# A fused linear-attention and squared-ReLU kernel: the order of the first 16 microseconds rewritten

## The chip, the cores and the metric

The kernel runs on one core of one Trainium2 chip. The metric is device time in microseconds (us) for one execution. The core has five engines with queues of their own: TensorE (PE in the profile; PEld is its weight load), VectorE (DVE), ScalarE (ACT), GpSimd (POOL) and SyncE (SP), which issues most of the DMAs. Each works through its own list of instructions in order and waits on semaphores for the others.

## The reference

```python
x = A_x                                  # 1 x 2048 x 448, bf16
xn = _layernorm(x, axis=-1)
s = _A_ref(xn, A_wqkv, A_wo)             # 16 heads of 28, linear attention
g = _silu(_B_ref(xn, B_w1, B_b1, B_w2, B_b2))
return x + s * g

# _A_ref: q, k, v from xn @ wqkv; phi(t) = where(t > 0, t + 1, exp(t)) + 1e-6
#   num = phi(q) (phi(k)^T v), den = phi(q) . sum phi(k); o = num / den; o @ wo
# _B_ref: h = xn @ w1 + b1; r = max(h, 0)^2; r @ w2 + b2       (448 -> 1792 -> 448)
```

## The kernel before

The 2048 tokens lie on 128 partitions as 16 tiles of 128; four tiles make a group g. The 448 features are three blocks of 128 rows and a tail of 64 rows. The hidden layer h of the second branch has 1792 columns in 14 chunks of 128 (index `fi`). Weights w1 come in four pieces of 512 columns (`load_w1(p)`), each as one load of the three full blocks, `("w1", p, 0)`, and two small loads of the 64-row tail, `("w1", p, 1)` and `("w1", p, 2)`, one in each half of the partitions. Two 64-row matmuls on different halves run side by side.

No loop order is left to a compiler. The program records operations (`add`) with what they read and write, an estimated duration and an engine. TensorE and SP keep the order in which the operations were recorded. For VectorE, ScalarE and GpSimd, `schedule` makes the order: of the operations that can start soonest it takes the one with the lowest `late`, its due time, worked back from TensorE's needs, or `prio` where one is set (lower goes first; within `pr.hot` operations get a rising series from -100). It also gives each accumulator (`Buf`) one of eight PSUM banks, the one that comes free soonest in its own estimate. The order is then fixed; on the chip an engine waits where the estimate was too early.

The head works as follows. For chunks 0 to 7 of group 0, h is computed from raw x, since the layer norm's mean and deviation can be put in afterwards. `warm` runs 34 dummy matmuls on zeros. `raw_transpose(lo)` turns two raw x tiles by TensorE into PSUM; VectorE and ScalarE copy two feature blocks each into `xr`. `pe_part(us, part, need)` multiplies chunks 0 to 3 for one half (256 tokens) of the group: 12 full-height matmuls and 4 of the 64-row tail. `col_sums(p)` sums the columns of w1 on TensorE; ScalarE (`csh`) and VectorE (`csl`) put them in a row form. `ln_stats`, `ln_rstd` and `ln_norm` are the layer norm: mean and variance on VectorE, Ln and Exp on ScalarE, the normalised tile `xn` on VectorE. `x_transpose` then copies the tail once more (VectorE) and issues a DMA transpose into `xT` on SP, two tiles at a time; all work after chunk 7 uses `xT`. `stat_rows` writes mean and deviation of the first four tiles into `rows`, `row_transpose` turns them on TensorE, and VectorE copies them to `rowT`. `aug` adds the product of `csl` and `rowT` to each accumulator of h, which puts mean and bias right, and hands the chunk to ScalarE (relu) and VectorE or ScalarE (square). `pe_two(a, b)` computes two chunks whole, with their tails side by side; `pe_main` and `pe_tails` are its two pieces.

The recorded order of TensorE in the head is: dummies, raw transposes of tiles 0 and 1, of 2 and 3, the two parts of chunks 0 to 3, column sums of pieces 0 and 1, chunks 4 and 6, row transpose, full blocks of chunk 5, augmentation of chunks 0 to 3, full blocks of chunk 7, tails of 5 and 7, augmentation of chunks 4 to 7, a transpose of b1, and then K (`kk`, with `phi`) and further chunks of h over `xT`. SP's recorded order is: x tiles 0 to 3, w1 piece 1, x tiles 4 to 7, b1, the k columns of wqkv, w1 piece 2, the two DMA transposes of tiles 0 to 3, the q columns (3 loads), w1 piece 3 (3 loads), x tiles 8 to 11, the transposes of tiles 4 to 7, x tiles 12 to 15, w2 and the rest. ScalarE issues w1 piece 0 and the row of b1.

Some lines of the profile: L425 DMA loads, L482 and L483 statistics, L490 and L494 Ln and Exp, L501 normalise, L510 tail copy, L515 DMA transpose, L614 and L621 phi on VectorE, L631 K, L653 Q, L680 and L683 relu, L688 square, L707 partial matmuls, L710 whole raw chunks, L711 chunks over `xT`, L731 to L734 raw transposes, L741 and L746 their copies, L767 to L776 column sums, L784 and L789 `csh` and `csl`, L803 to L826 `rows`, L842 row transpose, L849 its copy, L856 augmentation, L1193 dummies, L1247 and L1248 b1's transpose and copy.

Of the kernel before, what the change touches and what calls it, by code (L numbers as in the profile page):

```python
# [9 lines left out]
P = 128  # L10
S, D, F = 2048, 448, 1792
# [17 lines left out]
class Op:  # L29
    def __init__(self, eng, emit, reads, writes, dur, alts, nbytes):  # L30
        self.eng, self.emit, self.dur, self.alts, self.nbytes = eng, emit, dur, alts, nbytes
        self.reads, self.writes = list(reads), list(writes)
        self.raw, self.deps, self.succ = set(), set(), []
        self.start = self.end = None
        self.seq = None
        self.late = 1e9
        self.prio = None
        self.sync = None
        self.fence = False
        self.fixed = 0.0  # L40


class Program:
# [42 lines left out]
    def schedule(self):  # L86
# [34 lines left out]
        def ready(op):  # L121
            r = 0.0
            for d in op.deps:
                if d.end is None:
                    return None
                r = max(r, d.end + LAT)
            return r

        def bank_time(b):
# [11 lines left out]
        n = len(ops)  # L141
# [146 lines left out]
def bass_recurrent_scan__linear_attn_block__dense_activation_squared_relu__prompt_kernel(  # L288
    nc, A_x, A_wqkv, A_wo, B_x, B_w1, B_b1, B_w2, B_b2, out
):  # L290
    with ExitStack() as es:
# [3 lines left out]
        add = pr.add  # L295
# [128 lines left out]
        def dma(eng, dst, src, writes, nbytes, reads=(), dur=0.45):  # L424
            op = add(eng, lambda e, _: e.dma_start(dst, src), reads, writes, dur, nbytes=nbytes)  # L425
            if eng == "act":
                op.prio = -1000.0 + len(pr.ops)

        def load_x(lo, hi, eng="sp"):
            dma(eng, x_tok[:, lo:hi, :], tok(A_x, lo, hi), [("x", i) for i in range(lo, hi)], (hi - lo) * P * D * 2)  # L430

        def load_k(eng, w, src, name, lo, hi):
# [12 lines left out]
        def load_w1(p, eng, eng2):  # L445
            lo, hi = 512 * p, min(512 * p + 512, F)
            m = (hi - lo) // 2
            dma(
                eng, w_1[:, :, lo:hi], B_w1[0:384, lo:hi].rearrange("(c p) j -> p c j", p=P), [("w1", p, 0)],
                768 * (hi - lo),  # L450
            )
            for i in (0, 1):
                dma(
                    eng2, w_1r[64 * i : 64 * i + 64, 256 * p : 256 * p + m],
                    B_w1[384:448, lo + m * i : lo + m * i + m], [("w1", p, 1 + i)], 128 * m,
                )

        w1names = lambda p: [("w1", p, i) for i in range(3)]

# [3 lines left out]
        dma("act", b1row[:, :], B_b1.rearrange("(o f) -> o f", o=1), ["b1row"], F * 2)  # L463
        load_w1(1, "sp", "sp")
        load_x(4, 8)
        dma("sp", b1r[:, :], B_b1.rearrange("(f p) -> f p", p=P), ["b1r"], F * 2)
        load_k("sp", w_qkv, A_wqkv, "wk", D, 2 * D)
        load_w1(2, "sp", "sp")

        def late_loads():  # L470
# [10 lines left out]
        def ln_stats(si):  # L481
            add("dve", lambda e, _: e.bn_stats(st6[:, si, :], x_tok[:, si, :]), [("x", si)], [("st", si)], 0.58)  # L482
            add("dve", lambda e, _: e.bn_aggr(mv[:, si, :], st6[:, si, :]), [("st", si)], [("mv", si)], 0.15)  # L483

        def ln_rstd(lo, hi):
            c = slice(lo, hi)
            ts = range(lo, hi)
            add(
                "act",
                lambda e, _: e.activation(out=vep[:, c], in_=mv[:, c, 1], func=AF.Ln, bias=eps5[:, 0:1]),  # L490
                [("mv", i) for i in ts] + ["eps5", "actw"], [("vep", i) for i in ts], 0.25,
            )
            add(
                "act", lambda e, _: e.activation(out=rstd[:, c], in_=vep[:, c], func=AF.Exp, scale=-0.5),  # L494
                [("vep", i) for i in ts], [("rstd", i) for i in ts], 0.2,
            )
# [89 lines left out]

        def pe_part(us, part, need):
            def f(e, _):
                for u in us:
                    for k in range(3):  # L590
                        u[2](e, slice(0, 128), k, k == 0, False, part)
                for i in (0, 1):
                    us[i][2](e, slice(0, 64), 3, False, False, part)
                    last = us[2 + i][2](e, slice(64, 128), 3, False, False, part)
                return last

            banks = [u[0] for u in us]
            add("pe", f, list(need) + us[0][1] + (banks if part else []), banks, 14 * MM(256) + 0.1)

        def pe_tails(a, b, close=True):  # L600
            def f(e, _):
# [93 lines left out]
        def hh(g, fi, full=True):  # L695
            b = Buf("H")

            def mm(e, rw, c, start, stop, part=None):
                if c < 3:
                    lhs = w_1[rw, c, fi * P : (fi + 1) * P]  # L700
                else:
                    lhs = w_1r[rw, rest_col(fi) : rest_col(fi) + P]
                if raw(g, fi):
                    src = xr[rw, c, :]
                    if part is not None:
                        t = slice(256 * part, 256 * part + 256)
                        return e.matmul(  # L707
                            ps(b)[:, t], lhs, src[:, t], start=start and part == 0, stop=False, skip_group_check=True
                        )
                    return e.matmul(ps(b)[:, 0:512], lhs, src, start=start, stop=stop)  # L710
                return e.matmul(  # L711
                    ps(b)[:, 0:512], lhs, xT[rw, 4 * g : 4 * g + 4, c, :], start=start, stop=stop
                )
# [41 lines left out]
        def col_sums(p):  # L755
# [4 lines left out]
            def f(e, _):  # L760
# [22 lines left out]
            add(  # L783
                "act", lambda e, _: e.activation(out=csh[0:n, w : w + P], in_=ps(b)[0:n, w : w + P], func=AF.Copy), [b],  # L784
                [("csh", p)], 0.3,
            ).prio = -50
            add(
                "dve",
                lambda e, _: e.scalar_tensor_tensor(  # L789
# [4 lines left out]
            ).prio = -50  # L794

        def stat_rows():
            mvs = [("mv", i) for i in range(4)]
# [14 lines left out]
                ),  # L812
                mvs + ["rows0"], ["rows1"], 0.12,
            )
            add(
                "act",
                lambda e, _: e.activation(out=sdev[:, :], in_=vep[:, 0:4], func=AF.Exp, scale=0.5),
# [8 lines left out]
                lambda e, _: e.tensor_tensor(out=rows[:, :, :, 4], in0=sd4, in1=rows[:, :, :, 3], op=ALU.subtract),  # L826
                ["sdev", "rows3"], ["rows4"], 0.12,
            )
            add(
                "act",  # L830
                lambda e, _: e.activation(out=rvar[:, :], in_=vep[:, 0:4], func=AF.Exp, scale=-1.0),
# [3 lines left out]
        def row_transpose():  # L835
            b = Buf("R")

            def f(e, _):
                v = ps(b)[:, :].bitcast(bf)
                last = None  # L840
                for k in range(4):
                    last = e.transpose(  # L842
                        v[:, k * P : (k + 1) * P], rows[:, k, :, :].rearrange("p r j -> p (r j)"), ident[:, :]
                    )
                return last

            add("pe", f, ["rows1", "rows4", "ident"], [b], 0.3)
            v = ps_bf(b)
            add("dve", lambda e, _: e.tensor_copy(rowT, v()[:, 0:512]), [b], ["rowT"], 0.42).prio = -60  # L849

        def aug(units, fis, skip=False):
            def f(e, _):
# [287 lines left out]
        def ss_last(early, mid):  # L1140
# [43 lines left out]
            main(1)  # L1184
            main(2)

        def warm(n, after=()):
            b = Buf("W")

            def f(e, _):  # L1190
                last = None
                for _i in range(n):
                    last = e.matmul(ps(b)[:, 0:P], wz[:, :], wz[:, :], start=True, stop=True)  # L1193
                return last

            add("pe", f, ["wz", *after], [b], n * 0.06)

        def quads(what):
            us = []
# [6 lines left out]
            if us:  # L1206
                pe_two(*us)

        def ln(lo, hi, stats=True, step=2, lead=0.0):
            pr.lead = lead  # L1210
            if stats:
                for si in range(lo, hi):
                    ln_stats(si)
            ln_rstd(lo, hi)
# [132 lines left out]
```

## Time and profile before

| | us |
|---|---|
| median of 9 runs | 154.95 |
| lowest and highest | 154.56, 155.53 |
| the profiled execution | 154.95 |
| its span, first to last instruction | 153.2 |

The span leaves 1.75 us of the profiled execution's time outside. The granted clock of TensorE averages 1.000 over the span.

| engine | busy us | share of the span | instructions |
|---|---|---|---|
| PE | 146.5 | 96% | 1093 |
| DVE | 96.6 | 63% | 237 |
| ACT | 78.4 | 51% | 149 |
| POOL | 35.4 | 23% | 54 |

A row of the timeline has the start, the length, the engine, the line, the operation, its output and inputs, and how many were merged; in brackets the idle time of the engine before it and what ended that. The length of a merged row runs to the end of its last instruction; matmuls overlap, so the distance from start to start is what one costs. A row of the chain of waits has start, length and what it was. A busy share by slice is in tenths.

### The profile page before, as it was taken

Reading aid. Unit: us, or ns where it says so; the run is one execution under the profiler, and the core shown is the slowest. Engines: PE = TensorE matmul, PEld = TensorE weight load, DVE = VectorE, ACT = ScalarE, POOL = GpSimd, SP = SyncE. Lnnn points to the kernel's source line nnn. Section 1 sums busy time; section 2 is a strip of 40 time slices with the busy share of each in tenths; the row PEclk is TensorE's granted clock in tenths of the full one; section 3 lists DMA queues with packets and bytes.
Section 4 is the critical chain, followed back from the end, with each engine's and each line's share of the span. In section 5 each row is a group of like instructions: output and inputs, shape, how many; then the busy total and the mean of one; then the engine's idle time right before and its main releaser. Section 6 shows DMA issues by size and latency. Waiting matters only on the chain.

```text
span 153.2 us, 2797 instructions
## 1 busy us (share of the span) xinstructions
PE 146.5 (96%) x1093; PEld 69.4 (45%) x1093; DVE 96.6 (63%) x237; ACT 78.4 (51%) x149; POOL 35.4 (23%) x54
## 2 busy tenths in 40 slices
PE   7799999999999999999999999989999999999990
PEld 7564343444434444344443554434444545454450
DVE  2497959999998876364789510087954423414573
ACT  1531986887959598273969214979231021111100
POOL 7860004465000055000550000000005505133100
PEclk9999999999999999999999999999999999999999
DMA  4999799970007070000000000000001111010132
GB/s 114 334 277 135 191 257 307 319 163 7 0 0 135 2 140 1 0 0 4 0 2 2 4 0 0 0 4 0 0 0 46 44 34 60 0 60 0 60 109 71
DMA packets 17994, 11.05 MB, mean 72 GB/s; under 512 B 9469, under 2 KB 17597, under 8 KB 17982
## 3 DMA queue, kind: packets, MB, share of 16 engines
q1 hardware_dynamic: 17420, 10.42, 26.7%
q10 hardware_dynamic: 562, 0.46, 0.9%
q8 instruction: 8, 0.13, 0.3%
q14 instruction: 4, 0.03, 0.1%
HBM read 6.95 MB, written 1.84 MB: 57 GB/s over the span
## 4 chain that ended last, share of the span: by engine, by line
PE 72%; DVE 16%; DMA 5%; SPq 3%; ACT 1%; issue 1%; DVEq 0%
PE pb L1061 27%; PE pb L711 17%; PE pb L875 6%; DMA x_tok<-in_A_x_dram 5%; PE pb L1115 5%; PE pb L631 4%; PE pb L653 3%; DVE r L688 3%; DVE pk L621 3%; DVE st L482 3%; SPq L425 2%; PE pb L707 2%; DVE pqT L621 2%; DVE pk L614 2%; PE pb L1120 1%; DVE pqT L614 1%
## 5 line engine op out<-in xcount | busy, mean ns | idle before, releaser
L1061 PE MATMUL pb<-w,r 128*128 128x448 bf16 x224 | 44.8, 353 | 0.0
L711 PE MATMUL pb<-xT,w 64*128 64x512 bf16 (+1 forms) x264 | 36.9, 377 | 0.5 <-DVE kvm L915 0.4
L683 ACT ACTIVATE r<-pb,b1f 128x512 bf16<-128x512 f32 x48 | 29.7, 692 | 7.9 <-PE pb L711 7.8
L1061 PEld LDWEIGHTS pb<-w,r 128*128 128x128 bf16 x224 | 20.8, 98 | 20.9 <-issue 2.1
L688 DVE TENSOR_TENSOR r<-r 128x512 bf16<-128x512 bf16 x37 | 17.2, 501 | 12.1 <-ACT r L683 12.1
L1101 ACT ACTIVATE gbuf<-gbuf 128x448 bf16<-128x448 bf16 x15 | 8.6, 581 | 29.6 <-DVE gbuf L1091 29.6
L641 POOL TENSOR_TENSOR zacc<-zacc,pk 128x448 f32<-128x448 f32 x13 | 14.6, 1121 | 39.0 <-DVE pk L621 35.7
L1134 POOL TENSOR_TENSOR obuf<-obuf,x_tok 128x448 bf16<-128x448 bf16 x10 | 10.1, 1029 | 52.8 <-DVE obuf L1131 52.8
L711 PEld LDWEIGHTS pb<-xT,w 64*128 64x128 bf16 (+1 forms) x264 | 13.3, 94 | 17.9 <-issue 1.2
L1091 DVE TENSOR_TENSOR gbuf<-pb,b2b 128x448 bf16<-128x448 f32 x11 | 6.9, 625 | 16.1 <-PE pb L1061 16.0
L631 PE MATMUL pb<-w_qkv,xT 64*128 64x448 bf16 x112 | 13.2, 350 | 0.3 <-DVE b1f L1248 0.3
L1131 DVE TENSOR_TENSOR obuf<-pb,gbuf 128x448 bf16<-128x448 f32 x14 | 8.3, 621 | 5.3 <-PE pb L1120 5.2
L609 ACT ACTIVATE pk<-pb 128x448 bf16<-128x448 f32 x16 | 7.9, 548 | 7.1 <-PE pb L631 7.1
L482 DVE BATCH_NORM_STATS2 st<-x_tok 128x6 f32<-128x448 bf16 x16 | 9.5, 615 | 3.0 <-DMA x_tok<-in_A_x_dram 3.0
L689 ACT ACTIVATE r<-r 128x512 bf16<-128x512 bf16 x19 | 11.2, 643 | 0.0
L653 PE MATMUL pb<-xT,w_qkv 64*128 64x512 bf16 (+1 forms) x72 | 10.0, 377 | 0.3 <-DVE pk L621 0.3
L621 DVE SCALAR_TENSOR_TENSOR pk<-pb,pk 128x448 bf16<-128x448 f32 x16 | 9.6, 619 | 0.3
L875 PE MATMUL pb<-pk,xn 128*128 128x448 bf16 x48 | 9.4, 353 | 0.0
L711 PE MATMUL pb<-xT,w_1r 64*128 64x512 bf16 x48 | 9.1, 378 | 0.0
L1115 PE MATMUL pb<-msb,pqT 128*128 128x448 bf16 x42 | 9.1, 353 | 0.0
L631 PEld LDWEIGHTS pb<-w_qkv,xT 64*128 64x128 bf16 x112 | 5.2, 94 | 6.5 <-issue 0.7
L621 DVE SCALAR_TENSOR_TENSOR pqT<-pb,pqT 128x512 bf16<-128x512 f32 x12 | 8.0, 685 | 0.2
(127 smaller groups left out, 142.4 us busy)
## 6 DMA issues: line engine op xcount, KB each, us to landing
out_dram<-obuf SPq DMA_DIRECT2D x15, 112.0 KB, 1.7
w<-in_B_w_dram SPq DMA_DIRECT2D x1, 1568.0 KB, 10.3
x_tok<-in_A_x_dram SPq DMA_DIRECT2D x3, 448.0 KB, 5.4
w_qkv<-in_A_wqkv_dram SPq DMA_DIRECT2D x3, 336.0 KB, 5.6
w<-in_B_w_dram SPq DMA_DIRECT2D x2, 384.0 KB, 6.3
x_tok<-in_A_x_dram SPq DMA_DIRECT2D x2, 224.0 KB, 3.8
w_o<-in_A_wo_dram SPq DMA_DIRECT2D x1, 392.0 KB, 10.0
w<-in_B_w_dram ACTq DMA_DIRECT2D x1, 384.0 KB, 4.2
```

The lines of the kernel that those rows point to most:

```text
L482: add("dve", lambda e, _: e.bn_stats(st6[:, si, :], x_tok[:, si, :]), [("x", si)], [("st", si)], 0.58)
L621: lambda e, _: e.scalar_tensor_tensor(out=slot, in0=ps(buf)[:, 0:n], scalar=1.0 + 1e-6, in1=slot, op0=ALU.add, op1=ALU.max),
L631: return e.matmul(ps(b)[:, 0:D], xT[rw, si, c, :], w_qkv[rw, c, D : 2 * D], start=start, stop=stop)
L641: lambda e, _: e.tensor_tensor(out=o[:, :], in0=pk[:, 0, :] if i == 1 else zacc[:, :], in1=pk[:, i, :], op=ALU.add),
L653: return e.matmul(ps(b)[:, 0:512], w_qkv[rw, c, m * P : (m + 1) * P], xT[rw, 4 * g : 4 * g + 4, c, :], start=start, stop=stop,)
L683: rl = lambda e, _: e.activation(out=slot, in_=ps(b)[:, 0:512], func=AF.Relu, bias=b1f[:, fi : fi + 1])
L688: return e.tensor_tensor(out=slot, in0=slot, in1=slot, op=ALU.mult)
L689: return e.activation(out=slot, in_=slot, func=AF.Square)
L711: return e.matmul(ps(b)[:, 0:512], lhs, xT[rw, 4 * g : 4 * g + 4, c, :], start=start, stop=stop)
L875: last = e.matmul(ps(b)[:, 0:D], xn[:, si, c * P : (c + 1) * P], pk[:, si, :], start=(si == 0), stop=(si == NT - 1),)
L1061: last = e.matmul(ps(bb[fi >= 8])[:, 0:D], r2[:, fi, si * P : (si + 1) * P], w_2[:, fi, :], start=(fi == 0 and part is None) or (g == 0 an ...
L1115: last = e.matmul(ps(b)[:, 0:D], pqT[:, c, si * P : (si + 1) * P], msb[:, c, :], start=(c == 0), stop=False)
```

## The change

The diff does the following.

- `warm` issues 38 dummies instead of 34, always on one accumulator, and its estimate for the planner is 0.1 us each.
- `pe_part` does only the 12 full-height matmuls and waits only for the main load of w1 piece 0. The tails of chunks 0 to 3 follow as two `pe_tails` pairs over all 512 tokens, after the second part.
- TensorE's order behind that is: column sums of piece 0, row transpose, column sums of piece 1, augmentation of chunks 0 to 3, chunks 4 and 6 whole, chunks 5 and 7 whole, augmentation of chunks 4 to 7.
- The statistics of all four tiles of group 0 are recorded first, then `stat_rows` (with one Ln over four tiles), then the Exp for the normalisation, over four tiles, then the normalisations and both DMA transposes. In `stat_rows` the deviation comes ahead of that Exp and the variance's Exp behind it.
- The priorities of `csh` and `csl` go from -50 to -150, that of `rowT` from -60 to -200.
- The statistics of tiles 4 to 7 get a `hold`: the planner starts them no earlier than the copy of `rowT`.
- On SP the load of b1 comes behind the k columns. `load_w1r` is split off `load_w1`. Two further helpers (`load_x2`, `load_w1a`) are defined and not called.

```diff
             for d in op.deps: ...
+            for d in op.hold:
+                if d.end is None:
+                    return None
+                r = max(r, d.start)
...
         load_x(4, 8)
+        load_k("sp", w_qkv, A_wqkv, "wk", D, 2 * D)
         dma("sp", b1r[:, :], B_b1.rearrange("(f p) -> f p", p=P), ["b1r"], F * 2)
-        load_k("sp", w_qkv, A_wqkv, "wk", D, 2 * D)
...
         def pe_part(us, part, need):
             def f(e, _):
+                last = None
                 for u in us:
                     for k in range(3):
-                        u[2](e, slice(0, 128), k, k == 0, False, part)
-                for i in (0, 1):
-                    us[i][2](e, slice(0, 64), 3, False, False, part)
-                    last = us[2 + i][2](e, slice(64, 128), 3, False, False, part)
+                        last = u[2](e, slice(0, 128), k, k == 0, False, part)
                 return last
-            add("pe", f, list(need) + us[0][1] + (banks if part else []), banks, 14 * MM(256) + 0.1)
+            add("pe", f, list(need) + [("w1", 0, 0)] + (banks if part else []), banks, 12 * MM(256) + 0.1)
...
+            ln_vep(0, 4)
             add("act", ... sdev ...)
             add("dve", ... rows3 ...)
             add("dve", ... rows4 ...)
+            ln_rstd(0, 4, False)
             add("act", ... rvar ...)
...
-        warm(34)
+        warm(38)
         raw_transpose(0)
         raw_transpose(2)
         pe_part([H0[i] for i in range(4)], 0, [("xr", 0, 0), ("xr", 0, 1)])
         pr.hot = -100.0
-        for si in (0, 2):
-            ln(si, si + 2)
+        for si in range(4):
+            ln_stats(si)
         stat_rows()
+        ln(0, 4, stats=False, rstd=False)
         pr.hot = None
         pe_part([H0[i] for i in range(4)], 1, [("xr", 2, 0), ("xr", 2, 1)])
+        pe_tails(H0[0], H0[2], close=False)
+        pe_tails(H0[1], H0[3], close=False)
         col_sums(0)
+        rt = row_transpose()
         col_sums(1)
+        aug([H0[i] for i in range(4)], range(4), True)
         pe_two(H0[4], H0[6], close=False)
-        row_transpose()
-        pe_main(H0[5])
-        aug([H0[i] for i in range(4)], range(4), True)
-        pe_main(H0[7])
-        pe_tails(H0[5], H0[7], close=False)
+        pe_two(H0[5], H0[7], close=False)
         aug([H0[i] for i in range(4, 8)], range(4, 8))
...
-        ln(4, 8, lead=3)
+        ln(4, 8, lead=3, hold=[rt])
```

More of the change, by code (lines that the diff above doesn't have):

```diff
@@ L40, in __init__ @@
         self.fixed = 0.0
+        self.hold = ()
 class Program:
@@ L430, in load_x, with load_x2, load_w1a, load_w1r @@
             dma(eng, x_tok[:, lo:hi, :], tok(A_x, lo, hi), [("x", i) for i in range(lo, hi)], (hi - lo) * P * D * 2)
+        halves = (("sp", slice(0, 64)), ("act", slice(64, P)))
+        def load_x2(lo, hi):
+            for i, (eng, r) in enumerate(halves):
+                dma(
+                    eng, x_tok[r, lo:hi, :], tok(A_x, lo, hi)[r], [("x", k, i) for k in range(lo, hi)],
+                    (hi - lo) * 64 * D * 2,
+                )
+            for k in range(lo, hi):
+                pr.alias(("x", k), [("x", k, 0), ("x", k, 1)])
+        def load_w1a():
+            for i, (eng, r) in enumerate(halves):
+                dma(
+                    eng, w_1[r, :, 0:512], B_w1[0:384, 0:512].rearrange("(c p) j -> p c j", p=P)[r],
+                    [("w1", 0, 0, i)], 384 * 512,
+                )
+            pr.alias(("w1", 0, 0), [("w1", 0, 0, 0), ("w1", 0, 0, 1)])
+        def load_w1r(p, eng2):
+            lo, hi = 512 * p, min(512 * p + 512, F)
+            m = (hi - lo) // 2
+            for i in (0, 1):
+                dma(
+                    eng2, w_1r[64 * i : 64 * i + 64, 256 * p : 256 * p + m],
+                    B_w1[384:448, lo + m * i : lo + m * i + m], [("w1", p, 1 + i)], 128 * m,
+                )
         def load_k(eng, w, src, name, lo, hi):
@@ L451, in load_w1 @@
             )
-            for i in (0, 1):
[L453 to L456, printed above, removed]
+            load_w1r(p, eng2)
         w1names = lambda p: [("w1", p, i) for i in range(3)]
@@ L479, in bass_recurrent_scan__linear_attn_block__dense_activation_squared_relu__prompt_kernel, with ln_stats, ln_vep @@
         late_constants()
-        def ln_stats(si):
-            add("dve", lambda e, _: e.bn_stats(st6[:, si, :], x_tok[:, si, :]), [("x", si)], [("st", si)], 0.58)
+        def ln_stats(si, hold=()):
+            op = add("dve", lambda e, _: e.bn_stats(st6[:, si, :], x_tok[:, si, :]), [("x", si)], [("st", si)], 0.58)
+            op.hold = hold
             add("dve", lambda e, _: e.bn_aggr(mv[:, si, :], st6[:, si, :]), [("st", si)], [("mv", si)], 0.15)
-        def ln_rstd(lo, hi):
+        def ln_vep(lo, hi):
             c = slice(lo, hi)
@@ L492, in ln_rstd @@
             )
+        def ln_rstd(lo, hi, vep_=True):
+            c = slice(lo, hi)
+            ts = range(lo, hi)
+            if vep_:
+                ln_vep(lo, hi)
             add(
@@ L588, in f @@
             def f(e, _):
+                last = None
                 for u in us:
                     for k in range(3):
-                        u[2](e, slice(0, 128), k, k == 0, False, part)
-                for i in (0, 1):
-                    us[i][2](e, slice(0, 64), 3, False, False, part)
-                    last = us[2 + i][2](e, slice(64, 128), 3, False, False, part)
+                        last = u[2](e, slice(0, 128), k, k == 0, False, part)
                 return last
             banks = [u[0] for u in us]
-            add("pe", f, list(need) + us[0][1] + (banks if part else []), banks, 14 * MM(256) + 0.1)
+            add("pe", f, list(need) + [("w1", 0, 0)] + (banks if part else []), banks, 12 * MM(256) + 0.1)
         def pe_tails(a, b, close=True):
@@ L709, in mm @@
                         )
-                    return e.matmul(ps(b)[:, 0:512], lhs, src, start=start, stop=stop)
+                    return e.matmul(ps(b)[:, 0:512], lhs, src, start=start, stop=stop, skip_group_check=fi < 4)
                 return e.matmul(
@@ L785, in col_sums @@
                 [("csh", p)], 0.3,
-            ).prio = -50
+            ).prio = -150
             add(
@@ L793, in col_sums @@
                 [b, ("csh", p), "rmask"], [("csl", p)], 0.28,
-            ).prio = -50
+            ).prio = -150
         def stat_rows():
@@ L848, in row_transpose @@
             v = ps_bf(b)
-            add("dve", lambda e, _: e.tensor_copy(rowT, v()[:, 0:512]), [b], ["rowT"], 0.42).prio = -60
+            op = add("dve", lambda e, _: e.tensor_copy(rowT, v()[:, 0:512]), [b], ["rowT"], 0.42)
+            op.prio = -200
+            return op
         def aug(units, fis, skip=False):
@@ L1185, in ss_last @@
             main(2)
+        wb = Buf("W")
         def warm(n, after=()):
-            b = Buf("W")
             def f(e, _):
@@ L1192, in f @@
                 for _i in range(n):
-                    last = e.matmul(ps(b)[:, 0:P], wz[:, :], wz[:, :], start=True, stop=True)
+                    last = e.matmul(ps(wb)[:, 0:P], wz[:, :], wz[:, :], start=True, stop=True)
                 return last
-            add("pe", f, ["wz", *after], [b], n * 0.06)
+            add("pe", f, ["wz", *after], [wb], n * 0.1)
         def quads(what):
@@ L1207, in quads, with ln @@
                 pe_two(*us)
-        def ln(lo, hi, stats=True, step=2, lead=0.0):
+        def ln(lo, hi, stats=True, rstd=True, step=2, lead=0.0, hold=()):
             pr.lead = lead
@@ L1212, in ln @@
                 for si in range(lo, hi):
-                    ln_stats(si)
-            ln_rstd(lo, hi)
+                    ln_stats(si, hold)
+            if rstd:
+                ln_rstd(lo, hi)
             for si in range(lo, hi, step):
```

## The prediction

> **What bounds the kernel now.** I read the busy shares by slice first, then the chain of waits that ended last, then the first 25 us instruction by instruction.
>
> ```profile
> PE   7799999999999999999999999989999999999990
> DVE  2497959999998876364789510087954423414573
> ```
>
> (The slices are 3.83 us each.) TensorE looks like the bound everywhere, so time taken out of the head would seem to shorten the whole. But VectorE is full in the slices from 23 to 46 us as well. The chain, cut to 17 to 44 us (start, length, what), says which of the two sets the time there:
>
> ```profile
> 17.75 3.83 DMA x_tok<-in_A_x_dram
> 21.57 0.02 issue
> 21.59 0.63 DVE st L482
> 22.22 0.36 DVE pk L614 x2
> 22.58 1.06 DVE pk L621 x2
> ...
> 43.26 0.05 issue
> 43.31 0.82 PE pb L711 x5
> ```
>
> From 21.59 to 43.26 us the chain stays on VectorE, and TensorE takes it over only at 43.31. What starts it is the load of x tiles 8 to 11 that SP issues at 17.75. The same chain before that (12 to 18 us) runs over SP's queue: the second normalised-x transpose (12.78 to 14.08), then seven loads behind it, each 0.49 to 0.60. So between 13 and 43 us there are two nearly equal bounds. TensorE's last matmul before 43.31 starts at 42.85 and a 512-column matmul takes 0.216 (start to start in this trace), so TensorE alone would be there at 43.07: only 0.24 us of slack. After 43 us VectorE has idle time and the chain is TensorE's.
>
> The wait in question, in the timeline of VectorE and TensorE:
>
> ```profile
> 21.59 0.63 DVE L482 BATCH_NORM_STATS2 st<-x_tok 128x6 f32<-128x448 bf16 x1 [1.54 <-DMA x_tok<-in_A_x_dram]
> 23.17 0.98 PEld L653 LDWEIGHTS pb<-xT,w_qkv 128*128 128x128 bf16 x6 [0.75 <-DVE pk L621]
> ```
>
> VectorE sat 1.54 us idle because the planner put tile 8's statistics ahead of the first two k tiles' phi; the first Q matmuls then waited for the second of these for 0.41 us (0.63 start to start against 0.216).
>
> **The head, part by part.** The rows I use:
>
> ```profile
> 7.68 1.47 PE L707 MATMUL pb<-xr,w 128*128 128x256 bf16 x12 [0.79 <-ACT xr L746]
> 9.09 0.39 PE L707 MATMUL pb<-xr,w_1r 64*128 64x256 bf16 x4
> 14.31 0.42 DVE L849 COPY scr<-pb 128x512 bf16<-128x512 bf16 x1 [0.84 <-PE pb L842]
> 15.30 1.09 ACT L680 ACTIVATE r<-pb 128x512 bf16<-128x512 f32 x2 [2.75 <-PE pb L856]
> 10.24 3.83 SPq L515 DMA_TRANSPOSE xT<-xn  x2
> ```
>
> *Dummies, 34 to 38.* The trace grants the full clock from 4.15 us, 3.10 after the first dummy; the last dummies are 0.055 apart, the early ones 0.107. Four more cost 0.22 by the row. [...]
>
> *Tails out of the partial matmuls.* The row of the first part names ScalarE, but its sequencer stood until 7.52 at two DMA semaphores: the 64-row remainder of w1, landed at 7.48. The new part waits for the main w1 load (landed 5.02) and the copies of xr (ScalarE's, 0.60, done at about 6.35). It then follows the raw transposes: last one issued 6.65, plus 0.21 for the change of shape (as at 9.08), so 6.86 instead of 7.68. Twelve matmuls at 0.109 twice give 9.48. Tails cost 0.42 a part now (8.99 to 9.41), 0.84 together; two 512-column pairs cost 0.10 + 0.22 + 0.32 (13.45 to 13.56, one pair, 13.56 to 13.88) = 0.64. Column sums of chunks 0 to 3 start at about 10.13 (now 11.15), end at 10.63.
>
> *Statistics rows.* All four tiles' statistics come first. VectorE reaches the last at 8.55 as now; its aggregate ends near 9.37 (now 10.05). Then ScalarE, from the rows at 10.09 to 10.8: Ln to 9.71, deviation to 9.94. VectorE: rows3 to 10.18, by the planner's rule one normalisation (0.38), rows4 to 10.7. The row transpose runs at 10.75, its copy 11.2 to 11.62, the first column-sum row (0.35) to 11.9, and the early augmentation at 12.0 (copy to matmul is 0.12 now). TensorE, done with the second column sums at 11.48, waits 0.5 us here, and the pairs of chunks 4 to 7 stand behind that wait though they could run; today they cover it. So what the head gains before 10.75 isn't all passed on. If rows4 goes ahead of, or behind one more, normalisation: 11.7 or 12.4.
>
> *Early augmentation, both pairs whole.* After 12.0 + 0.32: two blocks of 1.73 (as 12.15 to 13.88), the second augmentation 0.23, b1's transpose 0.2: first K matmul at about 16.2, now 16.97 (that block now holds the row transpose 0.23, the wait for its copy, two augmentations, and a wait for b1f of 0.32 because its bank is reused; four banks are free by then). ScalarE's relu begins near 12.5, not 15.30. Gain on TensorE 0.75 at K, 0.84 behind it (0.09 of waiting on relu goes), and 1.25 at the first Q if its 0.41 goes too.
>
> *Normalised x.* Here the change takes something back. Its first two tiles wait for all four statistics and the row copy: the first DMA transpose is released at about 12.1 (now 10.24), the second at 12.83. SP issues in order. One takes 1.30 to 1.35 us at best (rows at 12.78, 18.38, 47.27), 2.48 at worst (10.24, while loads filled the queue until 13.39). I take the low end, since that 2.48 ended at 12.72, when the loads were nearly through: 12.1 + 1.33 + 0.05 + 1.30 = 14.78, now 14.08. [...] The rows decide: SP comes 0.70 late. Landing (1.85 after the issue) 16.6, needed at 17.0 by the first H over xT; 0.4 of slack. Behind it on SP are three wq, three w1 and x tiles 8 to 11: these land near 22.3, not 21.57. Statistics of tiles 4 to 7 (10.45 to 15.80 now) are held until the row copy and then run from about 13.0 to 15.4: no loss, for their transposes stand behind the x load on SP anyway. Moving b1r behind wk moves a 3.5 KB load and costs nothing.
>
> **The sum.** TensorE alone gains 1.25. VectorE: restart 0.70 later, but what it has left then is less. With relu finished by 18.3 the two exponentials of K come at 18.3 to 19.3, not 19.57 to 20.6, and the planner, which puts x 8 to 11 near 21 us in its own times, then finds K's phi ready first. That is 0.36 + 1.06 = 1.42 us of VectorE work (chain lines above) moved into the idle time. Net 1.42 - 0.70 = 0.72 at 43.31, the smaller gain, and it carries to the end. The profiled execution took 154.95 (span 153.2 and 1.75 around it), which is also the median: **154.2**.
>
> **Rivals.**
> *TensorE's whole gain* (1.25, 153.7): VectorE's full stretch holds work that nothing is waiting for yet (1.59 us of later statistics at 38.20, squares); a better order could hide it. Against it: no gap in 21 us.
> *Given back* (154.95): the planner reorders all that follows and 0.7 us is two fillers in a bad place.
> *SP's late x load makes it slower*: if the first transpose's issue takes 2.48 again, the second ends at 15.93, x 8 to 11 land 1.85 late, and even with phi first the sum is 1.85 - 1.42 = 0.43 worse, 155.4. If the planner leaves the statistics first, 0.70 late means 155.65. It decides from the point where the second transpose's issue ends later than 14.08 + 1.42 = 15.50. For it: the chain runs through that queue today.
> *The dummies don't matter*: already open at 4.15 in this execution; then nothing changes in the sum, as it counts nothing for them.
>
> **Numbers.** The sum as worked out 0.42 (its own range 153.9 to 154.6); whole gain 0.16; given back 0.15; slower by SP 0.27. Runs of this kernel can tell about 0.2% (0.31 us). Faster 0.42 + 0.16 = 0.58, same 0.15, slower 0.27. Range 153.4 (0.3 beyond the whole gain, for waits that go elsewhere) to 155.7.
>
> **What would show it.** First partial matmul near 6.9; column sums near 10.1; early augmentation near 12.0; first K near 16.2; second transpose's issue ends near 14.8; VectorE's statistics of tile 8 after the first two phi, with the wait for Q gone; the chain's change from VectorE to TensorE near 42.6. I am wrong if x tiles 8 to 11 land after 23, if these statistics still stand ahead of phi, or if the clock opens after the raw transposes.

## The result, and the profile after

The changed kernel takes 153.52 us (median of 12 runs, 153.44 to 154.49); the kernel before, timed beside it, 154.88. The ratio is 0.9918, with a 95% interval of 0.9900 to 0.9936: 1.36 us by the medians. In the profiled executions it is 1.44 (154.95 to 153.51; spans 153.22 and 151.78). The forecast was 154.2, a gain of 0.75; its range holds the result close to its lower end. The direction and the head came out as worked out; the gain is nearly twice the forecast. The outcome that lay nearest was "TensorE's whole gain", 153.7. A profile is of one execution, and executions of one kernel differ by 1 us and more (153.44 to 154.49 for the changed kernel, 154.49 to 156.37 for the one before), so a start read from a profile is weighed against the spans of all its runs.

The page of the changed kernel, busy shares by slice (3.79 us each), and the shares of its chain of waits:

```profile
PE   7999999999999999999999999989999999999990
...
DVE  2489849999997875455789310196954432414573
...
PE 96%; DVE 2%; ACT 0%; issue 0%; DVEq 0%
```

TensorE's second slice is full now. VectorE still has six slices at 9 from 23 us on, and yet the chain has 2% of VectorE in it, where the chain before had 16% (and 72% of TensorE). The stretch on VectorE from 21.59 to 43.26 has left the chain, although VectorE does nearly the same work there. The chain of the changed kernel in that stretch (start, length, what):

```profile
11.26 0.42 DVE scr L885
11.69 0.27 DVE scr L823
...
21.95 1.72 PE pb L687 x8
...
40.96 4.97 PE pb L745 x36
```

Only the copy of the row transpose (L849 before, L885 now) and the first column-sum row (L789, now L823) stand between matmuls; from 12 us to beyond 45 there is nothing but TensorE. The timeline of the head answers the rows of before (line numbers moved by 30 to 40):

```profile
7.00 2.79 PE L741 MATMUL pb<-xr,w 128*128 128x256 bf16 x24
...
12.00 0.39 PE L894 MATMUL pb<-scr 32*128 32x512 bf16 x4 [0.27 <-DVE scr L823]
12.08 2.72 SPq L551 DMA_TRANSPOSE xT<-xn  x2
...
12.45 2.06 ACT L714 ACTIVATE r<-pb 128x512 bf16<-128x512 f32 x4 [0.39 <-PE pb L894]
...
16.10 0.93 PE L665 MATMUL pb<-w_qkv,xT 64*128 64x448 bf16 x8
...
19.71 1.15 DVE L655 SCALAR_TENSOR_TENSOR pk<-pb,pk 128x448 bf16<-128x448 f32 x2
...
21.88 1.79 PE L687 MATMUL pb<-xT,w_qkv 128*128 128x512 bf16 x8
...
22.83 0.63 DVE L511 BATCH_NORM_STATS2 st<-x_tok 128x6 f32<-128x448 bf16 x1 [1.97 <-DMA x_tok<-in_A_x_dram]
```

Partial matmuls at 7.00, augmentation at 12.00, relu at 12.45, K at 16.10 (16.97 before), Q at 21.88 without a wait (23.17 before). VectorE waits longer for x tiles 8 to 11 than before, 1.97 us against 1.54, but both of the first phi now stand ahead of that wait and Q no longer depends on it.

### The profile page after: what moved, and what is told of

It reads as the page before. It is cut to its first block, busy times and chain, and to the rows that moved or that the text cites. A ratio compares the mean times of both kernels' runs of the same rounds, so it can differ in the third digit from the quotient of the medians.

```text
span 151.8 us, 2795 instructions
## 1 busy us (share of the span) xinstructions
PE 146.5 (97%) x1093; PEld 70.1 (46%) x1093; DVE 94.4 (62%) x234; ACT 79.8 (53%) x150; POOL 35.3 (23%) x54
## 4 chain that ended last, share of the span: by engine, by line
PE 96%; DVE 2%; ACT 0%; issue 0%; DVEq 0%
PE pb L1099 29%; PE pb L745 25%; PE pb L665 7%; PE pb L687 6%; PE pb L913 6%; PE pb L1153 5%; PE pb L1231 3%; PE pb L744 3%; PE pb L741 2%; PE pb L702 1%; PE pb L1158 1%; PE pb L999 1%; PE pb L919 1%; PE pb L942 1%; DVE obuf L1208 1%; PE pb L765 1%
## 5 line engine op out<-in xcount | busy, mean ns | idle before, releaser
L722 DVE TENSOR_TENSOR r<-r 128x512 bf16<-128x512 bf16 x34 | 16.2, 508 | 12.1 <-ACT r L717 12.0
L723 ACT ACTIVATE r<-r 128x512 bf16<-128x512 bf16 x22 | 12.9, 643 | 0.0
L648 DVE TENSOR_SCALAR pk<-pk 128x448 bf16<-128x448 bf16 x16 | 5.7, 360 | 3.9 <-ACT pk L643 3.6
```

Source lines behind the costliest of these rows:

```text
L722: return e.tensor_tensor(out=slot, in0=slot, in1=slot, op=ALU.mult)
L723: return e.activation(out=slot, in_=slot, func=AF.Square)
```

## The experiments

The first theory was the prediction's own: two bounds from 21.6 to 43.3 us, TensorE's, which starts with Q, and VectorE's, which starts when x tiles 8 to 11 land. Its rival was that TensorE alone counts and all of VectorE's stretch follows the start of Q. The first five experiments are meant to move one of the two without the other; the first does so only in part.

### Before, with the tails part alone

The edit to `pe_part` of the diff, and behind its second call:

```diff
+        pe_tails(H0[0], H0[2], close=False)
+        pe_tails(H0[1], H0[3], close=False)
```

> The kernel before with one part of the change: the 64-row tails of chunks 0 to 3 out of the partial matmuls, and the first part waiting for the main load of w1 alone. TensorE reaches the column sums about 1.0 us earlier (10.1 instead of 11.15) and, if nothing holds it, K at about 16.0. Two-bounds theory (between 21.6 and 43.3 us VectorE sets the time, started by the landing of x tiles 8 to 11): that landing stays at 21.6, tile 8's statistics stay ahead of the first phi, the first Q stays near 23.2 and the hand-over near 43.3, so 154.9, no change. TensorE-alone theory (the gain is simply time taken out of TensorE's head): 1.0 us less, 153.9.

Measured: 154.95, ratio 0.9989 (0.9963 to 1.0014), so no gain: the time of the two-bounds theory, but not its path. Its chain of waits:

```profile
15.45 0.98 ACT r L678 x2
...
16.48 0.93 PE pb L629 x8
...
21.72 0.98 ACT pk L607 x2
22.70 1.17 ACT r L681 x2
...
23.97 1.78 PE pb L651 x8
```

K comes at 16.48, 0.49 earlier than before, but Q at 23.97, 0.80 later. The augmentation is still late (13.99), so ScalarE's relu of the first chunks holds K until 16.44. Q then waits 1.64 us for ScalarE alone: its accumulator is here one that comes free behind two relus (22.70 to 23.86), where it came free with VectorE's phi before. These relus stand behind two exponentials of K, ahead of which ScalarE is idle for 0.70 us, so at Q it is ScalarE's order and not a backlog that holds TensorE. In the same execution x tiles 8 to 11 landed at 22.38, 0.81 later than before, and the first phi behind them ended at 23.87; Q would have been late by that path too. So this profile doesn't tell the two theories apart, and its span, 153.95, lies above the median of its twelve runs, 153.2, which is that of the kernel before. What the times do show is that the head's gain on TensorE alone doesn't reach the end.

### Before, with x tiles 8 to 11 loaded early

SP issues that load ahead of the q columns; all orders of the other engines stay.

```diff
         pr.schedule()
+        q = pr.order["sp"]
+        x8 = next(o for o in q if o.writes[0] == ("x", 8))
+        wq = next(o for o in q if o.writes[0] == ("wq", 0))
+        q.remove(x8)
+        q.insert(q.index(wq), x8)
...
```

> The kernel before, where SP alone issues the load of x tiles 8 to 11 ahead of the q columns; every engine's order stays as it was. It lands near 18 us instead of 21.57. Two-bounds theory: VectorE no longer waits 1.54 us, Q's wait of 0.41 and the wait at 43.31 (0.24) go, then TensorE alone is the bound: 154.25. TensorE-alone theory: only Q's 0.41, 154.5. If the wait merely moves to the q columns, which land later: 154.9.

Measured: 154.7, ratio 0.9992 (0.9967 to 1.0018). The load lands at 17.73 instead of 21.57, nearly 4 us earlier, and by the interval takes at most 0.33% off. That excludes the 0.70 us of the two-bounds theory (154.25), not the 0.45 of the other (154.5). The chain shows why:

```profile
28.10 0.59 PE pb L631 x6
...
28.71 0.55 ACT pk L609
...
29.29 0.29 DVE pk L614
...
43.11 3.08 PE pb L711 x23
```

VectorE no longer waits for x, and TensorE still takes over at 43.11 (43.31 before). VectorE's part of the chain begins at 29.29, after 1.16 us without work, released by the exponential of a K product that TensorE finished at 28.69. What the chain before told as one stretch from the landing on had a second origin behind it, in TensorE's own pace. Q starts at 22.97 here, and from there to the hand-over it is 20.14 us, exactly as before (23.17 to 43.31).

### After, with tile 8's statistics ahead of the first phi

```diff
+        q = pr.order["dve"]
+        st8 = next(o for o in q if o.writes[0] == ("st", 8))
+        pk1 = next(o for o in q if o.writes[0] == ("pk", 1))
+        q.remove(st8)
+        q.insert(q.index(pk1), st8)
...
```

> The changed kernel, where tile 8's statistics stand ahead of the first phi in VectorE's order, as before the change; all else is kept. They wait for the landing at 22.8. Two-bounds theory: phi 2.5 us later, first Q near 24.4 instead of 21.9, and VectorE loses the 1.4 us it had moved ahead: 155.4 to 156.0, slower than before the change. If VectorE's place in the order didn't matter: 153.5.

Measured: 156.64, ratio 1.0115 (1.0083 to 1.0148), slower than the kernel before. Its chain:

```profile
19.49 3.98 DMA x_tok<-in_A_x_dram
...
23.49 0.63 DVE st L511
24.12 0.36 DVE pk L648 x2
24.48 0.54 DVE pk L655
...
25.07 1.79 PE pb L687 x8
```

That is beyond the 155.4 to 156.0 expected. Q comes at 25.07, 3.19 later than in the changed kernel, and the span is 3.19 longer (154.97): all of it is passed on. Of that, 0.75 are there at K already (16.85), since the clock opened at 6.86 us in this execution and at 4.91 in the changed kernel's; the wait at Q is 2.37. VectorE's order at this one place is worth more than the whole change, and the rival that ended slower was a matter of this order.

### After, with x tiles 8 to 11 later, and earlier

The later one has the load on SP behind the first transpose of tiles 4 to 7; the earlier one is the edit made above to the kernel before.

```diff
...
+        t4 = next(o for o in q if o.writes[0] == ("xT", 4))
+        q.remove(x8)
+        q.insert(q.index(t4) + 1, x8)
...
```

> The changed kernel, where SP issues the load of x tiles 8 to 11 behind the first transpose of tiles 4 and 5, so that it lands about 1.3 us later (24.1); every engine's order is kept. If VectorE is still about tied with TensorE at the hand-over near 41.9 (0.10 us of waiting there): 1.0 to 1.2 us slower, 154.6. If TensorE alone sets the changed kernel's time and VectorE has over 1 us to spare: 153.5.

> The changed kernel, where SP alone issues the load of x tiles 8 to 11 ahead of the q columns, so that it lands near 18.8 us instead of 22.8. If TensorE is now the bound throughout: 153.4 to 153.5 (at most the 0.10 us of waiting at 41.9). If VectorE still holds it back: about 153.0.

Measured: later 154.64, 0.9970 (0.9952 to 0.9989); earlier 153.76, 0.9885 (0.9840 to 0.9930), whose interval holds the changed kernel's 0.9918. The load lands at 24.57, 22.81 (changed kernel) and 18.71. In the later one TensorE waits twice:

```profile
26.17 0.93 PE L665 MATMUL pb<-w_qkv,xT 64*128 64x448 bf16 x8 [0.30 <-DVE pk L655]
...
43.15 0.82 PE L745 MATMUL pb<-xT,w 64*128 64x512 bf16 x6 [0.27 <-DVE pqT L655]
```

The engine's idle times are 0.30 and 0.27; from start to start the two places lose 0.47 and 0.43. The time is the one expected if VectorE were about tied with TensorE (154.6), but the tie is not exact. The clock opened later in this execution (5.94 us against 4.91) and Q came 0.48 later; counted from Q, the load landed 1.28 later than in the changed kernel (2.21 us behind Q against 0.93), and from Q to the end it took 0.80 longer. So at 22.8 the landing has about 0.5 us in hand, an estimate from these two profiles; a later one is a bound. Four us earlier brings nothing that shows: from Q to the hand-over it is 20.00 us with the load at 22.81 and at 18.71.

### After, with the augmentation covered

The prediction had TensorE waiting 0.5 us for the augmentation while chunks 4 and 6 could run. This places them ahead of it.

```diff
-        aug([H0[i] for i in range(4)], range(4), True)
         pe_two(H0[4], H0[6], close=False)
+        aug([H0[i] for i in range(4)], range(4), True)
```

> The changed kernel with the augmentation of chunks 0 to 3 behind chunks 4 and 6, so that these cover the wait for the copied rows. TensorE's 0.5 us idle at 11.5 goes, K comes near 15.6 instead of 16.1; relu of chunks 0 to 3 starts about 0.8 us later. TensorE-bound: 153.0. If the early relu is what keeps K's phi ahead of tile 8's statistics, or the transposes' landing at 16.7 holds the first chunk over xT: 153.5 or more.

Measured: 153.83, ratio 0.9909 (0.9878 to 0.9940): no gain over 0.9918. From its chain:

```profile
13.94 3.33 DMA xT<-xn
...
17.31 1.04 PE pb L745 x8
```

The wait is gone, and the second DMA transpose's landing, 17.27, is what comes next: the first h over `xT` needs it. Its clock opened at 5.99 us; against the profile with x late, where it opened at 5.94, K is 0.25 earlier (16.33) and Q only 0.03 (22.33). A second version also takes tile 1's statistics ahead of the first copy of `xr` on VectorE, so that the rows and the transposes come sooner (landed 16.12):

```diff
...
-        for si in range(4):
-            ln_stats(si)
+        ln_stats(0).prio = -301.0
+        ln_stats(1).prio = -300.0
+        ln_stats(2)
+        ln_stats(3)
...
```

> A version meant to beat the changed kernel: the statistics of tile 1 ahead of the first copy of xr on VectorE (which waits idle there from 4.6 to 6.1 us), so that rows and both DMA transposes come about 0.45 to 0.9 us earlier, and the augmentation of chunks 0 to 3 behind chunks 4 and 6, which then cover the wait for the copied rows. First-Q theory (from the first Q on, the rest takes 130.0 us whatever the head did, and 1.7 lie around the span): K at 15.6, second transpose lands near 15.8, first Q near 21.4, so 153.1. VectorE theory (the time hangs on the landing of x tiles 8 to 11, here about 0.5 earlier): 153.0 as well, but with a wait near 42 us. If the transposes still hold the first chunk over xT: 153.5.

Measured: 153.41 (153.29 to 153.74), ratio 0.9899 (0.9876 to 0.9921). No wait is left in its head from the partial matmuls to Q, but the 153.1 of the first-Q theory isn't reached; in the profiled execution the clock opened at 6.57 us and Q came at 22.22, not 21.4. Its median is 0.11 below the changed kernel's, but the intervals overlap; that it is faster isn't shown.

### After, with 34 dummies

```diff
-        warm(38)
+        warm(34)
```

> The changed kernel with 34 dummies as before. By the sum the four dummies cost and bring nothing: 153.5 (the raw transposes of tiles 2 and 3 start at 5.8 instead of 6.0, and the rows, not they, set the augmentation at 12.0). If the clock's opening needs them (it opened at 4.9 in the changed kernel's profile, at 4.15 before): some executions 0.2 to 0.5 slower.

Measured: 153.68, ratio 0.9880 (0.9838 to 0.9921). In its profile the clock opens at 4.11 and the raw transposes follow at 4.40. The four dummies bring and cost nothing that can be measured.

### Before, with GpSimd's sum put off

VectorE's stretch in the kernel before has six squares that take 0.75 us each on average from start to start, and GpSimd's running sum of k (`zacc`) lies beside them. Here the first sum also waits for the last chunk of the second group, and the rest follow.

```diff
...
-                for i in range(1, 8):
-                    zsum(i)
...
-                for i in range(8, 12):
+                for i in range(1, 12):
                     zsum(i)
```

> The kernel before, where GpSimd's running sum of k tiles starts only after the last chunk of group 1, behind VectorE's full stretch. In that stretch of before, 14 of VectorE's min operations took 5.05 us start to start and 6 squares 4.50, overlapped by GpSimd for 6.6 us. If GpSimd's sum stretches them: min near 0.2 each and squares near 0.35, the stretch some 3 us shorter, but TensorE is only 0.24 us behind, so about 154.65. If the stretching has another cause: the same durations and 154.9.

Measured: 157.14, ratio 1.0108 (1.0071 to 1.0145), slower where 154.65 was expected. Groups of VectorE between 21.5 and 43.4 us (line, operation, shapes, count, busy us and mean ns, idle before), first of the kernel before, then of this one:

```profile
L688 DVE TENSOR_TENSOR r<-r 128x512 bf16<-128x512 bf16 x6 | 4.7, 829 | 0.0
...
L614 DVE TENSOR_SCALAR pk<-pk 128x448 bf16<-128x448 bf16 x8 | 3.3, 438 | 0.0
```

```profile
L688 DVE TENSOR_TENSOR r<-r 128x512 bf16<-128x512 bf16 x6 | 2.1, 412 | 0.0
L614 DVE TENSOR_SCALAR pk<-pk 128x448 bf16<-128x448 bf16 x8 | 2.0, 269 | 1.5 <-ACT pk L609 1.5
```

Without GpSimd beside it VectorE needs 2.6 us less for six squares and 1.3 less for eight of phi's minima. TensorE then takes over at 43.33, having started Q at 23.44: 19.89 us. So of the 20.14 before, 0.25 were VectorE's, as the prediction said of the slack (0.24). But the sums put off, from 49.2 to 57.0 us, fall on the normalisations of the third group, and TensorE waits:

```profile
57.97 0.82 PE L711 MATMUL pb<-xT,w 64*128 64x512 bf16 x6 [2.06 <-DVE pk L621]
```

That costs 2.06 us, far more than the 0.25, and the expectation had left it out.

### After, with one part taken back

First the tails go back into the two parts and these wait for all of w1 piece 0 again; then the recording order of statistics and rows goes back, with the rest of the change kept.

```diff
...
+                for i in (0, 1):
+                    us[i][2](e, slice(0, 64), 3, False, False, part)
+                    last = us[2 + i][2](e, slice(64, 128), 3, False, False, part)
...
-        pe_tails(H0[0], H0[2], close=False)
-        pe_tails(H0[1], H0[3], close=False)
...
```

> The changed kernel with the 64-row tails back in the partial matmuls and with the wait for the whole of w1 piece 0. First-Q theory: TensorE reaches the row transpose 0.9 later than now (11.7), since rows are ready before; augmentation 12.9, K 16.9, first Q 22.7: 154.4. If the rows, not TensorE, set the head: 153.6.

```diff
...
-            ln_vep(0, 4)
...
-            ln_rstd(0, 4, False)
...
-        for si in range(4):
-            ln_stats(si)
-        stat_rows()
-        ln(0, 4, stats=False, rstd=False)
+        for si in (0, 2):
+            ln(si, si + 2)
+        stat_rows()
...
```

> The changed kernel with the statistics and rows in their former order (two tiles at a time, the first transpose early, rows last). rows4 comes near 12.0 instead of 10.8, the augmentation near 13.2; the planner then puts tile 8's statistics ahead of the first phi again. First-Q theory: first Q near 23.2, as before the change: 154.9. If only the augmentation's delay counts: first Q 23.0, 154.7. If the earlier transposes make up for it: 153.5.

Measured: 154.8, 0.9985 (0.9964 to 1.0006), with Q at 22.74; and 155.32, 1.0037 (1.0005 to 1.0069), with Q at 23.08. With the tails back, the first partial matmul starts at 7.72 again (7.00 in the changed kernel). Several of its runs have 2.0 to 2.9 us outside the span instead of 1.7 or 1.8; by the spans the median is 152.65 against 151.8, 0.85 longer, as Q is 0.86 later. The chain of the second:

```profile
11.99 0.24 DVE rows L860
...
12.27 0.40 PE pb L876 x4
```

There TensorE stands at the row transpose for `rows`, which VectorE writes behind four normalisations. Tile 8's statistics are ahead of phi again, as expected, but the load lands at 21.21 and Q doesn't wait for them. The timed difference to the changed kernel, 1.2% by the two ratios or 1.8 us, is more than the 1.20 by which its profile's Q is later: the profile is the shortest of its twelve runs, whose spans go from 152.9 to 155.1 with a median of 153.6. Why they spread so far is open. By the starts of Q, tails are worth 0.86 us within the change and the order of the rows 1.20. They sum to 2.06, more than the 1.29 of the whole: without the tails part the rest moves Q by 0.43, without the row order by 0.09, and the tails part alone gains nothing in time (its profile has Q later). These are starts of single executions, whose clock opened at different moments, so they are rough.

### Q and the end, over all kernels

Span less the start of the first Q matmul, from the profiled executions, and the median span of all runs of the kernel:

| kernel | first Q | span | difference | median span |
|---|---|---|---|---|
| before | 23.17 | 153.22 | 130.04 | 153.2 |
| after | 21.88 | 151.78 | 129.90 | 151.8 |
| before, tails alone | 23.97 | 153.95 | 129.98 | 153.2 |
| before, x early | 22.97 | 153.02 | 130.05 | 152.9 |
| after, statistics first | 25.07 | 154.97 | 129.91 | 154.9 |
| after, x early | 21.62 | 151.54 | 129.92 | 152.05 |
| after, augmentation covered | 22.33 | 152.12 | 129.79 | 152.0 |
| the same with tile 1 first | 22.22 | 152.01 | 129.79 | 151.65 |
| after, 34 dummies | 21.65 | 151.68 | 130.02 | 151.9 |
| after, tails back | 22.74 | 152.81 | 130.07 | 152.65 |
| after, rows back | 23.08 | 152.87 | 129.78 | 153.6 |
| after, x late | 22.36 | 153.06 | 130.70 | 152.9 |
| before, sum put off | 23.44 | 155.46 | 132.02 | 155.45 |

Q starts anywhere from 21.6 to 25.1, and the end follows it at 129.8 to 130.1 us in eleven of thirteen. The two others are those in which a wait was put behind Q. From the matmul of the hand-over to the end it is 109.9 us in twelve of the thirteen, and from Q to that matmul 19.9 where TensorE nowhere waits; what lies above is waiting, 0.24 in the kernel before and 0.11 in the changed one. Hence the change in one line: Q 1.29 us earlier, 0.15 less behind it, 1.44 in the span. The 0.15 is the smaller part and not a firm one: with 34 dummies the same wait is 0.22.

## Why the prediction was right, and where it was not

**The head was right.** Foreseen and measured: partial matmuls 6.86 and 7.00, column sums 10.13 and 10.27, augmentation 12.0 and 12.00, ScalarE's relu near 12.5 and 12.45, K 16.2 and 16.10, the gain of TensorE up to Q 1.25 and 1.29. The column sums are late by the 0.14 of the first row, and augmentation isn't, since what it waits for is VectorE's copy and row. That it is on time to 0.01 us has luck in it. With four dummies more and the clock opening at 4.91 us instead of 4.15, the raw transposes of tiles 0 and 1 started at 5.00 (4.42 before) and those of tiles 2 and 3 at 6.00 and not 5.82. The forecast counts 0 for the four dummies: no run shows that at this place, where the two profiles are 0.18 apart; in the time of the whole, 38 and 34 can't be told apart (153.52 and 153.68). VectorE's last statistics came at 8.73 (8.55 foreseen), and the steps behind them were that much shorter than foreseen.

**The DMA transposes were right, by the rows.** The two issues end at 14.80 (14.78 foreseen) and cost 2.72 together; at the 0.59 us of the issue of x tiles 8 to 11 (the row at 18.47) they would have ended near 13.7, an estimate from these rows: the second can start only when VectorE's copy of the tails ends at 13.15. Tiles 8 to 11 landed at 22.81, 0.5 later than foreseen: the load was issued at 18.47 as the sum has it (0.72 later than before), and took 4.3 us instead of 3.83.

**The planner's choice was right**, both phi ahead of tile 8's statistics, and forcing the other order gave the slower outcome, at 156.64 by more than the 155.65 foreseen for it.

**What failed is the term of 0.72**, "Net 1.42 - 0.70 = 0.72 at 43.31, the smaller gain". It treats VectorE's stretch from the landing of x 8 to 11 to 43.26 as a bound with a start of its own, so that a landing later by 0.70 delays its end by 0.70 and only moved work shortens it. Both halves of the term are off.

The 0.70: the landing does not set the end. Four us earlier in the kernel before gained at most 0.33%, and 4 us earlier in the changed one nothing that shows. What it did cost in the kernel before was the wait at Q, 0.41, and only because the statistics stood ahead of phi. The work inside the stretch is released by TensorE, as the chain with x early shows at 28.7, and so the stretch moves with Q. In the changed kernel VectorE has caught up by the same place, though it restarts 1.24 us later than before (22.83 against 21.59), and waits for ScalarE, which waits for K:

```profile
28.63 0.28 DVE L648 TENSOR_SCALAR pk<-pk 128x448 bf16<-128x448 bf16 x1 [0.16 <-ACT pk L643]
```

The 1.42: from VectorE's restart to the hand-over it is 21.72 us before (21.59 to 43.31) and 19.05 after (22.83 to 41.88), 2.67 less. Two phi left the stretch, as foreseen. What the prediction put at nothing is GpSimd's sums: two pairs of VectorE's minima that were held up beside them before no longer are. One pair, at 26.60 before and 24.80 after, takes 0.49 us instead of 1.01; the other, before and after:

```profile
24.09 0.98 DVE L614 TENSOR_SCALAR pk<-pk 128x448 bf16<-128x448 bf16 x2
```

```profile
23.38 0.45 DVE L648 TENSOR_SCALAR pk<-pk 128x448 bf16<-128x448 bf16 x2
```

So VectorE, from 0.24 us too late at the hand-over, is 0.11 too late there, at 41.88 instead of the 42.6 foreseen, and in place of the 0.72 stands TensorE's 1.29 and 0.15 less of waiting for VectorE. The chain was read rightly, and a step too far was made from it: it names what came last in one execution, not what would be last if that were taken away. With two bounds 0.24 apart, the one the chain doesn't show was the one to follow. The range holds the result because it was drawn 0.3 beyond the whole gain, not because the sum was right.

**Rivals.** "TensorE's whole gain" was nearest, but its reason, squares and statistics in a better order, isn't what the traces show: six squares stand in the stretch before and after. "Given back" did not happen. "SP's late x load" needs a landing later than 22.8 us by about 0.5 or more, shown at 24.57 with 0.9 us of waits. That the dummies don't matter holds.

## What to carry to other kernels

Where the chain of waits stays long on a secondary engine that follows the bound engine closely (here by 0.24 of 153 us), move the supposed start of its stretch by itself before you put it into a sum: if 4 us earlier moves nothing, the stretch has another origin. Look for one instruction of the bound engine behind which the rest of the kernel is of constant length (here the first Q), and count a change first by when that one starts, then by any new wait behind it. Two parts that each feed the same instruction don't add up: neither is worth much until the later of them is early.

## What the runs showed of the hardware that was not expected

**The clock's opening moves from execution to execution.** The prediction read it at 4.15 us in one profile. In thirteen profiled executions TensorE's full clock is granted at 4.01 to 6.86 us, with the first dummy at the same place; five are at 5.9 or later, with 34 dummies and with 38 alike. That is 2.85 us from end to end, and what moves it isn't shown. With 38 dummies the raw transposes of tiles 2 and 3 start at 5.74 to 6.00 where the clock opens by 4.91, and at 6.48 to 6.68 where it opens at 5.94 or later; the augmentation of the changed order is then at 12.48 and 12.75 instead of 11.74 to 12.00. The 1.01 us from end to end is about the spread between 153.44 and 154.49, though no run shows the clock's opening and the time of many executions side by side, so that it is the cause isn't shown.

**GpSimd's sums hold VectorE up, one instruction at a time.** The means above mix two kinds. In the stretch of the kernel before three of the six squares last 0.41 us or less and three 1.25 or 1.26; of the 14 minima three last 0.80 to 1.10 and the others 0.29 or less. Each of the six long ones lies beside one of GpSimd's additions of f32 rows (1.03 to 1.27 us) and ends 0.13 to 0.29 us after it. One addition and the square beside it:

```profile
36.48 1.09 POOL L641 TENSOR_TENSOR zacc<-zacc,pk 128x448 f32<-128x448 f32 x1
36.61 1.25 DVE L688 TENSOR_TENSOR r<-r 128x512 bf16<-128x512 bf16 x1
```

With the sums put off, no square of the stretch lasts longer than 0.42 us, and the four normalisations beside which the sums then fall last 1.19 to 1.20 instead of 0.38. So it is these additions that hold VectorE up; by what mechanism isn't shown. In the changed kernel four instructions of the stretch are held up instead of six: the first sum (20.94 to 21.97) lies in VectorE's wait for x, and beside the two sums from 24.96 to 27.29 nothing on VectorE lasts longer than 0.69. The prediction did not reckon with it, and it is part of why VectorE had less to do than foreseen.
